# Moving casts to GpSimd and mirrors away from it in a fused attention and Fourier-mixing kernel

## The chip, the cores and the metric

The kernel runs on one core of one Trainium2 chip. The metric is the device time of one execution in microseconds (us). A core has five engines that run their own instruction streams in order: TensorE (PE: matmuls and transposes, its weight loads shown as PEld), VectorE (DVE), ScalarE (ACT), GpSimd (POOL) and SyncE (SP), which only issues transfers here. They wait for each other by semaphores. Transfers between the chip's memory (HBM) and the on-chip buffer (SBUF) run on 16 DMA engines, fed by queues: q1 holds what SyncE issues, q10 what ScalarE issues, q0 what GpSimd issues. Matmuls write to PSUM, a small accumulator memory that the kernel uses in banks.

## The reference

Inputs: q, k and v of 4 batches x 8 heads x 768 positions x 64, in float32, two weights (512x2048 and 2048x512), and two numbers, 8 global and 96 local positions.

```
scores = q @ k.T / sqrt(64)                     # per batch and head
keep   = (column < 8) or (0 <= row - column < 96)
scores = scores - slope[head] * distance        # then -1e9 where not keep
a      = softmax(scores)
x      = (a @ v), heads side by side            # 4 x 768 x 512
u      = x + real(fft(fft(x, axis=1), axis=2))
un     = (u - mean(u)) / sqrt(var(u) + 1e-6)    # over the last axis
out    = u + relu(un @ w_ch1) @ w_ch2
```

## The kernel before

**Two layers of work.** For each batch there is an attention part and a mixing part, and after them a large feed-forward part that fills TensorE. Heads are taken in pairs (hp 0 to 3); the number n = 4 * batch + hp names a pair through the whole kernel, so q4, k4 and v4 are batch 1's first loads and k7 its last k.

Attention, per pair: `load` reads q, k and v as float32 (L354 to L394). `cast_qk` (L400 to L421) casts q and k to float16, 128x768 each, with heads and positions put in another order. `trans` (L489) turns the cast tiles with 12 TensorE transposes ("pt") and copies them to SBUF as qkT (L505, L507). Two small GpSimd copies, kG (L512), take the global columns out of qkT. `score` (L519) has three units per pair ("sc"): four matmuls, an exponential on ScalarE (L566) into "er", a multiplication with a mask on VectorE (L581). `cast_v` (L465) casts v on GpSimd (L469). `v_global`, `glob` and `av` make the weighted sums ("pvg", "pgl", "pav"), which VectorE divides into x (L691, L692).

Mixing, per batch: `bounce` (L701) writes x to HBM (xd) and reads it back in another row order (xr). `fold_s` and `fold_d` (L723 to L856) fold x for the transform on VectorE. `y_unit` (L861) makes the transform along positions ("py"), copied out as zy (L896, L898). `mirror` (L911) makes copies with reversed columns of five parts of zy: r0 (three instructions, L916 to L918) and rn 0 to 3 (one each, L929 on ScalarE or L931 on GpSimd). `u_unit` (L952) makes the transform along features ("pu"), adds xr into u (L984), normalizes it (un, L1004 or L1006), squares it for the variance (L1013) and computes one over the deviation on GpSimd ("rstd", L1020 and L1021). `nt_unit` (L1025) transposes un ("ptu").

Feed-forward, per chunk c of 256 rows (three per batch): `ph_unit` (L1056) is the first product, 8 units of 8 matmuls, each copied out with the relu by ScalarE or VectorE (L1072, L1073); `pg_unit` (L1079) is the second, 16 matmuls of 512 columns per 128-row tile, closed by a VectorE step (L1100) that scales and adds u, and by the store (L1105).

**Buffers.** q and k of all pairs but batch 0's first three share three buffers (qs), v has two (vs), the cast tiles two (qk), xr and zy one each. A load waits until the cast has freed the buffer. Attention and mixing units share two PSUM banks ("xx"); the ph and pg units have two each.

**What sets the order.** The order is written by a planner in the kernel, `Plan` (L18 to L152), when the program is built. It keeps an expected time for each engine and each result. A piece of work for VectorE, ScalarE, GpSimd or SyncE is handed to `later` with its `ways`: the engines that may do it, each with an expected duration. `run` (L115) takes TensorE's units from four lists (mixing, attention, ph, pg), always the one that can start first, and places the other engines' work by the expected times. The hardware then executes every engine's list in that fixed order, whatever the real times are. `LAND` (L343) gives the planner the expected landing times of batch 1's and 2's loads. `fill` (L313) puts empty matmuls into early gaps.

**Queues around the change.** SyncE issues all loads of q, k and v, and from chunk 6 on the stores. Batch 1's loads wait until batch 0's xr has been issued; batch 2's wait for `hold` (L1188): a tiny transfer out of the second weight, which SyncE can issue only when that part of the weight (w2[1]) has landed. GpSimd issues the eight weight loads (`wload`, L1174), w1[0] to w1[3] and w2[0] to w2[3], between its casts and copies.

Of the kernel before, what the change touches and what calls it, by code (L numbers as in the profile page):

```python
# [14 lines left out]
P = 128  # L15
# [143 lines left out]
def act(n):  # L159
    return 0.19 + n / 1200.0  # L160
# [15 lines left out]
def kernel(  # L176
# [136 lines left out]
    def fill(until):  # L313
# [15 lines left out]
        for i in range(n):  # L329
# [10 lines left out]
    TT = {}  # L340


    LAND = {4: (43.5, 43.3, 47.3), 5: (51.6, 55.5, 54.0), 6: (57.4, 60.9, 59.2), 7: (65.9, 67.0, 64.9),  # L343
            8: (79.4, 81.6, 84.8), 9: (86.6, 91.0, 88.2), 10: (92.8, 96.3, 94.8), 11: (100.0, 102.5, 98.4)}

    def landed(n, w):
        def then(t):
# [5 lines left out]
    def load(b, hp, which):  # L353
        n = HP * b + hp  # L354
        h0 = 2 * hp
        vtag, vi = ("u", hp) if b == 0 else ("vs", n - HP)
        stage[("vs", n)] = (vtag, vi)
        gate = [("hold", b)] if b == 2 else [("xri", 0)] if b == 1 else []
        if which == "v" and b == 0:
            def run():  # L360
                t = buf(vtag, vi, [P, 2 * NS, Dh], FP32, 1)
                stage[("v", n)] = t
                qk_dma(t.rearrange("p (j t) d -> p j (t d)", t=2), v, b, h0)
            pl.later([("SP", 0.45, run)], free(vtag, vi), 0.0, [("ld", "v", n)], dma=1.34)
        elif which == "v":
            def run():
                t = buf(vtag, vi, [P, 2 * NS, Dh], FP32, 1)
                stage[("v", n)] = t
                src = v[b, h0:h0 + 2].rearrange("h s d -> (h s) d").rearrange("(n m t) d -> t m n d", m=64, t=2)
                for t2 in range(2):  # L370
                    nc.sync.dma_start(t[64 * t2:64 * t2 + 64], src[t2])
            pl.later([("SP", 0.9, run)], free(vtag, vi) + gate, 0.0, [("ld", "v", n)], lat=(0.0, 4.0, 6.0, 5.0)[b], dma=2.45, then=landed(n, 2))
        elif b == 0 and hp < 3:
            cell = {}

            def run(cell=cell):
                cell[0] = buf("hT", hp, [P, 2, NS, 2 * Dh], FP32, 2)
                for w, src in enumerate((q, k)):
                    qk_dma(cell[0][:, w], src, b, h0)
            pl.later([("SP", 0.9, run)], free("hT", hp), 0.0, [("ld", "qk", n, w) for w in range(2)], dma=2.68,  # L380
                     then=lambda t: pl.tok.__setitem__(("ld", "qk", n, 0), t - 1.34))
            for w in range(2):
                cast_qk(b, hp, w, lambda w=w, cell=cell: cell[0][:, w], ("hT", hp))
        else:
            for w, src in enumerate((q, k)):
                cell = {}
                i = 2 * (n - 3) + w

# [11 lines left out]
    def cast_qk(b, hp, w, src, freed):  # L400
        n = HP * b + hp

        def cast(on):
            if n not in qk16:
                qk16[n] = buf("qk", n, [P, 2, NS, 2, Dh], FP16, 1)
            d = qk16[n][:, w]
            s = src().rearrange("p (h i) (t d) -> p h (i t) d", h=2, t=2).rearrange("p h j d -> p j h d")
            if on == "ACT":
                A(d, s, AF.Copy)  # L409
            elif on == "DVE":  # L410
                V.tensor_copy(d, s)
            else:
                nc.gpsimd.tensor_copy(d, s)
        ways = [("ACT", act(768), lambda: cast("ACT")), ("DVE", dve2(768), lambda: cast("DVE"))]
        if b:
            ways = [("ACT", act(768), lambda: cast("ACT")), ("POOL", 1.6, lambda: cast("POOL"))]
        else:
            if hp:
                ways = ways[1:2] if w else [("POOL", 0.85, lambda: cast("POOL"))]
        pl.later(ways, [("ld", "qk", n, w)] + free("qk", n), 0.0, [("qk", n, w)], [("free",) + freed],  # L420
                 rank=1 if b else 0)  # L421
# [488 lines left out]

    def mirror(b):  # L911

        def r0():
            rev = buf("rev0", b, [P, 2, 2, P], FP16, 2)
            src = T[("y", b)][:, 4]
            nc.gpsimd.tensor_copy(rev[:, 0, :, 0:1], src[:, 0, :, 0:1])  # L916
            nc.gpsimd.tensor_copy(rev[:, 0, :, 1:P], src[:, 0, :, P - 1:0:-1])
            nc.gpsimd.tensor_copy(rev[:, 1], src[:, 1, :, ::-1])  # L918
            Y[(b, 0, 3, "r")], Y[(b, 3, 3, "r")] = rev[:, 0], rev[:, 1]
        pl.later([("POOL", 1.0, r0)], [("y", b, 0, 3), ("y", b, 3, 3)] + free("rev0", b), 0.0,  # L920
                 [("y", b, 0, 3, "r"), ("y", b, 3, 3, "r")], [("free", "zy", 2 * b + 1)])

        def rn(n, on):
            if n == 0:
                T[("rev", b)] = buf("ww", IW(b, NA(b) + 1), [P, 4, 2, 2, P], FP16, 1)
            rev = T[("rev", b)]
            d, y = rev[:, n], T[("y", b)][:, n, :, :, ::-1]
            if on == "ACT":
                A(d, y, AF.Copy)  # L929
            else:  # L930
                nc.gpsimd.tensor_copy(d, y)  # L931
            for a in range(2):
                Y[(b,) + YG[n // 2][2 * (n % 2) + a] + ("r",)] = rev[:, n, a]
        for n in range(4):
            ys = YG[n // 2][2 * (n % 2):2 * (n % 2) + 2]
            pl.later([("ACT", act(512), lambda n=n: rn(n, "ACT")), ("POOL", 1.0, lambda n=n: rn(n, "POOL"))],
                     [("y", b) + y for y in ys] + free("ww", IW(b, NA(b) + 1)) + [("rv", b, n - 1)][:n], 0.0,
                     [("y", b) + y + ("r",) for y in ys] + [("rv", b, n)],
                     [("free", "zy", 2 * b + 1)] if n == 3 else [])
# [139 lines left out]
    def pg_unit(c, t, part):  # L1079
# [26 lines left out]
            pl.later([("ACT" if c < 6 else "SP", 0.45, st)], [("ob", i)], 0.0, [], [("free", "ob", i)], lat=1.6, dma=0.7)  # L1106
        PG.append((needs, ("pg",) if part == 0 else None, run))


    def dma_const(dst, src, us, tok, needs=()):  # L1110
        pl.later([("SP", 0.45, lambda: nc.sync.dma_start(dst, src.ap()))], needs, 0.0, [tok], lat=0.2, dma=us)

    with tc.manual_schedule():
# [74 lines left out]
        def hold(n, src):  # L1188

            nc.sync.dma_start(dr.tile([1, 32], FP16, tag=f"hold{n}", name=f"hold{n}", bufs=1), src)  # L1190
        pl.later([("SP", 0.5, lambda: hold(2, w2[0:1, 4, 0:32]))], [("w2", 1)], 0.0, [("hold", 2)])
        for b in range(B):
            if b:
                for hp in range(HP):
# [96 lines left out]
```

## Time and profile before

| what | us |
|---|---|
| median of 7 runs (lowest to highest) | 280.87 (280.07 to 283.28) |
| the profiled execution, whole | 282.54 |
| its span, first to last instruction | 280.8 |
| PE busy, share of the span | 265.8, 95% |
| DVE busy | 178.9, 64% |
| ACT busy | 151.2, 54% |
| POOL busy | 61.3, 22% |
| q and k casts on ACT (L409), 20 times | 16.6 in all, 0.839 each |
| q and k casts on POOL (L413), 5 of qs | 5.3 in all, 1.057 each |
| v casts on POOL (L469), 12 times | 10.9 in all, 0.909 each |
| mirror copies rn on POOL (L931), 6 times | 4.0 in all, 0.668 each |
| last VectorE step of a tile (L1100) | 0.747 |
| last store, issue to landing | 2.1 |

How to read it: busy times overlap, and a share is an average over stages with different limits. The page has several views: busy times by engine; the span in 40 equal slices of 7.02 us, a digit for the busy tenths in each; the DMA queues; the chain of waits, followed back from the last instruction; the costliest groups of instructions. Further views of the same trace show instructions in order of time, busy time by stages, and what landed when. A row such as `L409 ACT ACTIVATE qk<-qs` names the source line, the engine, the operation and the tiles written and read. Line numbers are those of the kernel before.

### The profile page before, as it was taken

What the parts mean: (1) busy time and instruction counts of PE and PEld (TensorE: products, weight loads), DVE (VectorE), ACT (ScalarE), POOL (GpSimd) and SP (SyncE); (2) the same over time, 40 slices, a digit from 0 to 9 for tenths busy, and PEclk for the clock granted to TensorE, in tenths of its full rate; (3) what the DMA queues carried; (4) which work ended last, traced back from release to release, by engine and by line L of the source; (5) the groups of instructions that cost most, each with busy time, mean ns of one, the idle gap of its engine ahead of it and who ended that gap; (6) DMA issues with size and microseconds to landing.
All of it is one profiled execution on the core that took longest, in us unless ns stands there. A gap on an engine that the chain in (4) does not pass through costs nothing.

```text
span 280.8 us, 6109 instructions
## 1 busy us (share of the span) xinstructions
PE 265.8 (95%) x2505; PEld 179.6 (64%) x2505; DVE 178.9 (64%) x356; ACT 151.2 (54%) x245; POOL 61.3 (22%) x118
## 2 busy tenths in 40 slices
PE   8789998998699999999999999999999999999994
PEld 3445577886456556786885678666677577757441
DVE  4676937786357999976899565767895525111121
ACT  2878257892571368888547765684157346324000
POOL 1573535254112053262012102011002020000000
PEclk9999999999599999999999999999999999999999
DMA  7999799999989989982045110100540101010111
GB/s 220 291 284 288 170 266 204 210 212 216 235 154 193 307 242 245 239 175 74 1 121 163 75 40 0 41 0 4 153 146 37 41 37 40 0 75 20 57 75 75
DMA packets 63101, 38.10 MB, mean 136 GB/s; under 512 B 20450, under 2 KB 58594, under 8 KB 62946
## 3 DMA queue, kind: packets, MB, share of 16 engines
q1 hardware_dynamic: 51458, 25.66, 38.7%
q10 hardware_dynamic: 7392, 7.87, 9.2%
q0 software_dynamic: 4224, 4.19, 9.1%
q8 instruction: 19, 0.31, 0.5%
q14 instruction: 8, 0.07, 0.1%
HBM read 32.47 MB, written 9.44 MB: 149 GB/s over the span
## 4 chain that ended last, share of the span: by engine, by line
PE 72%; DMA 14%; DVE 5%; SPq 3%; issue 2%; ACT 2%; POOL 1%; ACTq 0%; POOLq 0%
PE pg L1089 29%; PE ph L1066 26%; DMA qs<-in_k_dram 7%; PE sc L543 3%; PE pav L672 3%; PE pt L498 3%; DMA vs<-in_v_dram 3%; SPq L398 2%; DMA qs<-in_q_dram 2%; PE pu L963 2%; DVE x L692 2%; PE py L879 2%; PE ptu L1035 1%; PE py L882 1%; DMA xd<-x 1%
## 5 line engine op out<-in xcount | busy, mean ns | idle before, releaser
L1066 PE MATMUL ph<-unT,w 128*128 128x256 f16 x768 | 95.5, 276 | 0.0
L1089 PE MATMUL pg<-w,hT 128*128 128x512 f16 x384 | 90.9, 379 | 0.0
L1066 PEld LDWEIGHTS <-w 128*128 128x128 f16 x768 | 72.9, 99 | 16.5 <-issue 4.4
L1072 ACT ACTIVATE hT<-ph 128x512 f16<-128x512 f32 x56 | 33.4, 597 | 47.9 <-PE ph L1066 47.6
L1089 PEld LDWEIGHTS <-hT 128*128 128x128 f16 x384 | 35.9, 98 | 35.7 <-issue 1.5
L1100 DVE SCALAR_TENSOR_TENSOR ob<-pg,sm,u 128x512 f32<-128x512 f32 x24 | 17.9, 747 | 41.6 <-PE pg L1089 41.3
L566 ACT ACTIVATE er<-sc 128x992 f16<-128x992 f32 (+2 forms) x42 | 38.1, 922 | 8.8 <-PE sc L543 6.6
L1073 DVE TENSOR_SCALAR hT<-ph 128x512 f16<-128x512 f32 x40 | 27.6, 690 | 18.9 <-PE ph L1066 18.6
L581 DVE TENSOR_TENSOR ex<-er,mk 128x992 f16<-128x992 f16 (+2 forms) x42 | 26.7, 647 | 4.4 <-ACT er L566 4.3
L984 DVE SCALAR_TENSOR_TENSOR u<-pu,xr 128x512 f32<-128x512 f32 x24 | 15.7, 686 | 8.6 <-PE pu L963 8.6
L409 ACT ACTIVATE qk<-qs 128x768 f16<-128x768 f32 x20 | 16.6, 839 | 7.7 <-DMA qs<-in_k_dram 6.3
L512 POOL COPY kG<-qkT 64x8 f16<-64x8 f16 x32 | 10.5, 327 | 41.9 <-DVE qkT L507 32.1
L498 PE MATMUL pt<-ident,qk 128*128 128x128 f16 x192 | 14.3, 227 | 5.1 <-ACT er L566 4.1
L692 DVE TENSOR_TENSOR x<-pav,rc 128x512 f16<-128x512 f32 (+1 forms) x27 | 17.1, 632 | 0.9
L543 PE MATMUL sc<-qkT 64*128 64x256 f16 (+1 forms) x192 | 16.6, 263 | 0.5 <-ACT v L460 0.4
L498 PEld LDWEIGHTS <-qk 128*128 128x128 f16 x192 | 12.4, 102 | 7.3 <-issue 5.1
L672 PEld LDWEIGHTS <-ex 128*128 128x128 f16 x352 | 15.0, 97 | 2.5 <-DVE rc L691 0.4
L672 PE MATMUL pav<-v,ex 128*128 128x65 f16 x352 | 16.1, 193 | 0.0
L896 ACT ACTIVATE zy<-py 128x512 f16<-128x512 f32 (+1 forms) x13 | 9.7, 759 | 11.8 <-DVE eA L829 5.2
L469 POOL CAST v<-vs 128x768 f16<-128x768 f32 x12 | 10.9, 909 | 22.9 <-DMA vs<-in_v_dram 22.8
L1013 ACT ACTIVATE un<-un 128x512 f16<-128x512 f16 x24 | 14.9, 622 | 1.7 <-PE ptu L1035 1.2
L507 DVE COPY qkT<-pt 128x1536 f16<-128x1536 f16 x14 | 13.4, 954 | 1.6 <-PE pt L498 1.4
(104 smaller groups left out, 290.6 us busy)
## 6 DMA issues: line engine op xcount, KB each, us to landing
qs<-in_q_dram SPq DMA_DIRECT2D x13, 384.0 KB, 7.1
qs<-in_k_dram SPq DMA_DIRECT2D x13, 384.0 KB, 6.4
vs<-in_v_dram SPq DMA_DIRECT2D x24, 192.0 KB, 7.5
w<-in_moe_w_ch_dram POOLq DMA_DIRECT2D x8, 512.0 KB, 10.4
out_dram<-ob ACTq DMA_DIRECT2D x12, 256.0 KB, 2.3
out_dram<-ob SPq DMA_DIRECT2D x12, 256.0 KB, 2.0
xd<-x ACTq DMA_DIRECT2D x12, 192.0 KB, 3.4
xr<-xd ACTq DMA_DIRECT2D x6, 384.0 KB, 3.8
```

What stands on the lines that cost most here:

```text
L409: A(d, s, AF.Copy)
L498: nc.tensor.transpose(o[:, j % 2], src[:, w, j].rearrange("p h d -> p (h d)"), idn)
L543: nc.tensor.matmul(pa[:, s, c0:c0 + cw], TT[n][lo:lo + 64, 1, i * P:(i + 1) * P], TT[n][lo:lo + 64, 0, i * P:i * P + cw], start=(not inps) ...
L566: A(mine(), cut(pa), AF.Exp, 0.0, 0.125)
L581: VT(o, mine(), m, op=ALU.mult)
L672: nc.tensor.matmul(po[:, jj, hh * 65:(hh + 1) * 65], lhsT, v16[b % 2][:, i, h, 0:65], start=(jp == 0 and a == 0), stop=(a == len(ops) - 1) ...
L692: VT(X[b][:, 2 * jp:2 * jp + 2, first * Dh:(first + nh) * Dh].rearrange("p j (h d) -> p j h d", d=Dh), pv[:, :, :, 0:Dh], rc.to_broadcast( ...
L1066: nc.tensor.matmul(ph[:, a * CH:(a + 1) * CH], w1[:, d, jb * P:(jb + 1) * P], UNT[c][:, d, :], start=(d == 0), stop=(d == ND - 1))
L1072: pl.later([("ACT", act(512), lambda: A(dst, ph, AF.Relu)), ("DVE", dve(512), lambda: V.tensor_scalar_max(dst, ph, 0.0))], [], e, [("h", c ...
L1073: ("DVE", dve(512), lambda: V.tensor_scalar_max(dst, ph, 0.0))],
L1089: nc.tensor.matmul(pg, HT[c][:, jb, t * P:(t + 1) * P], w2[:, jb, :], start=(jb == 0), stop=(jb == NJ - 1))
L1100: V.scalar_tensor_tensor(cell[0], pg, MV[c][:, t, 3:4], UT[c][:, t, :], op0=ALU.mult, op1=ALU.add)
```

## The change

Four edits, and new expected landing times for the planner.

1. The casts of q and k of batches 1 to 3 have GpSimd as their only way, with an expected 1.0 us. Before, ScalarE or GpSimd could be chosen.
2. The mirrors of batches 1 to 3 lose GpSimd as a way: r0 may go to ScalarE or VectorE, rn to ScalarE or VectorE. Batch 0 keeps what it had.
3. Batch 3's loads wait for a second `hold`, a tiny transfer out of batch 1's xr, queued on SyncE.
4. The last 128-row tile of the last chunk is done in two halves of 256 columns (`pg_last`): 16 matmuls, a VectorE step and a store each.

```diff
-    LAND = {4: (43.5, 43.3, 47.3), 5: (51.6, 55.5, 54.0), 6: (57.4, 60.9, 59.2), 7: (65.9, 67.0, 64.9),
-            8: (79.4, 81.6, 84.8), 9: (86.6, 91.0, 88.2), 10: (92.8, 96.3, 94.8), 11: (100.0, 102.5, 98.4)}
+    LAND = {4: (46.0, 46.0, 47.0), 5: (51.5, 55.5, 54.0), 6: (56.5, 60.0, 59.0), 7: (66.5, 68.0, 64.0),
+            8: (79.5, 81.0, 83.5), 9: (86.3, 89.5, 87.5), 10: (90.7, 95.7, 93.8), 11: (99.5, 101.5, 98.5)}
...
-        gate = [("hold", b)] if b == 2 else [("xri", 0)] if b == 1 else []
+        gate = [("hold", b)] if b > 1 else [("xri", 0)] if b == 1 else []
...
         if b:
-            ways = [("ACT", act(768), lambda: cast("ACT")), ("POOL", 1.6, lambda: cast("POOL"))]
+            ways = [("POOL", 1.0, lambda: cast("POOL"))]
...
-        def r0():
+        def r0(cp):
...
-            nc.gpsimd.tensor_copy(rev[:, 0, :, 0:1], src[:, 0, :, 0:1])
-            nc.gpsimd.tensor_copy(rev[:, 0, :, 1:P], src[:, 0, :, P - 1:0:-1])
-            nc.gpsimd.tensor_copy(rev[:, 1], src[:, 1, :, ::-1])
+            cp(rev[:, 0, :, 0:1], src[:, 0, :, 0:1])
+            cp(rev[:, 0, :, 1:P], src[:, 0, :, P - 1:0:-1])
+            cp(rev[:, 1], src[:, 1, :, ::-1])
...
-        pl.later([("POOL", 1.0, r0)], [("y", b, 0, 3), ("y", b, 3, 3)] + free("rev0", b), 0.0,
+        pl.later([("ACT", 1.0, lambda: r0(nc.scalar.copy)), ("DVE", 0.8, lambda: r0(V.tensor_copy))] if b else
+                 [("POOL", 1.0, lambda: r0(nc.gpsimd.tensor_copy))], [("y", b, 0, 3), ("y", b, 3, 3)] + free("rev0", b), 0.0,
...
-                nc.gpsimd.tensor_copy(d, y)
+                (V if on == "DVE" else nc.gpsimd).tensor_copy(d, y)
...
-            pl.later([("ACT", act(512), lambda n=n: rn(n, "ACT")), ("POOL", 1.0, lambda n=n: rn(n, "POOL"))],
+            pl.later([("ACT", act(512), lambda n=n: rn(n, "ACT")), ("DVE", 0.7, lambda n=n: rn(n, "DVE")) if b else ("POOL", 1.0, lambda n=n: rn(n, "POOL"))],
...
+    def pg_last(c, t, half):
...
+        cols = slice(half * 256, half * 256 + 256)
...
+            for jb in range(NJ):
+                nc.tensor.matmul(pg[:, 0:256], HT[c][:, jb, t * P:(t + 1) * P], w2[:, jb, cols],
+                                 start=(jb == 0), stop=(jb == NJ - 1))
...
+                V.scalar_tensor_tensor(cell[0], pg[:, 0:256], MV[c][:, t, 3:4], UT[c][:, t, cols],
+                                       op0=ALU.mult, op1=ALU.add)
...
+            pl.later([("SP", 0.45, lambda: nc.sync.dma_start(out[b].rearrange("(m r) d -> m r d", r=6)[:, rs, cols], cell[0]))],
+                     [("ob", i)], 0.0, [], [("free", "ob", i)], lat=1.6, dma=0.4)
...
         pl.later([("SP", 0.5, lambda: hold(2, w2[0:1, 4, 0:32]))], [("w2", 1)], 0.0, [("hold", 2)])
+        pl.later([("SP", 0.5, lambda: hold(3, XR[1][0:1, 5, 0:32]))], [("xr", 1)], 0.0, [("hold", 3)])
...
             for t in range(2):
+                if (c, t) == (NP * B - 1, 1):
+                    pg_last(c, t, 0)
+                    pg_last(c, t, 1)
+                    continue
```

Since the planner orders everything anew, the instruction lists of all engines differ from batch 1 on. The parts that the prediction uses: on GpSimd, between batch 0's rstd and batch 1's last kG, the list is now kG 4 (first half), cast q5, kG 4 (second), rstd 1, cast v5, cast k5, cast q6, cast v6, kG 5 (first), cast k6, kG 5 (second), w2[0], rstd 2, w2[1], cast v7, kG 6, w2[2], w2[3], cast q7, cast k7, kG 7. On SyncE, batch 1's loads come in the order q4, k4, v4, q5, v5, k5, q6, v6, k6, t1 (a table), v7, q7, k7, hold 2; before, q6 came ahead of k5. On TensorE the transposes of pair 4 stand after two ph units instead of before the first, and those of pair 7 have the third score unit of pair 6 and batch 1's global-value unit ahead of them instead of behind. The number of matmuls of each kind is the same, but for the last tile.

More of the change, by code (lines that the diff above doesn't have):

```diff
@@ L1107, in pg_unit, with run, add @@
         PG.append((needs, ("pg",) if part == 0 else None, run))
+    def pg_last(c, t, half):
+        b, pr = divmod(c, NP)
+        rs = PAIRS[pr][t]
+        cols = slice(half * 256, half * 256 + 256)
+        def run(start, ring):
+            pg = bank(ring, f"pg_{c}_{t}_{half}")
+            for jb in range(NJ):
+                nc.tensor.matmul(pg[:, 0:256], HT[c][:, jb, t * P:(t + 1) * P], w2[:, jb, cols],
+                                 start=(jb == 0), stop=(jb == NJ - 1))
+            e = pl.pe(mm_us(256, NJ), start)
+            i = HP + 2 * c + t + half
+            cell = {}
+            def add():
+                cell[0] = buf("ob", i, [P, 256], FP32, 1)
+                V.scalar_tensor_tensor(cell[0], pg[:, 0:256], MV[c][:, t, 3:4], UT[c][:, t, cols],
+                                       op0=ALU.mult, op1=ALU.add)
+            pl.later([("DVE", dve(256), add)], [("rstd", c)] + free("ob", i), e, [("ob", i)], ring=ring, rank=0)
+            pl.later([("SP", 0.45, lambda: nc.sync.dma_start(out[b].rearrange("(m r) d -> m r d", r=6)[:, rs, cols], cell[0]))],
+                     [("ob", i)], 0.0, [], [("free", "ob", i)], lat=1.6, dma=0.4)
+        PG.append(([("h", c, j) for j in range(NJ // 2)], ("pg", "ph"), run))
     def dma_const(dst, src, us, tok, needs=()):
```

## The prediction

> I call a load and its cast by pair of heads, counted through the batches (n = 4 x batch + pair): k7 is the k of the last pair of batch 1. w2[0] to w2[3] are the four loads of the second weight.
>
> **What bounds the kernel now.** First the page's slices of 7 us: TensorE is busy nearly throughout, with one hole and one stretch of low clock in the same place, slices 10 to 12.
>
> ```profile
> PE   8789998998699999999999999999999999999994
> ...
> PEclk9999999999599999999999999999999999999999
> DMA  7999799999989989982045110100540101010111
> ```
>
> After that place TensorE doesn't stop until the end, so time won or lost there arrives at the end one for one, unless another wait takes it back. Second, the table by stages (us; then busy us and instruction counts of PE, PEld, DVE, ACT, POOL; granted clock; DMA share; GB/s), cut at the hole:
>
> ```profile
> 64.00:69.17 5.17, 5.17 (x49) 3.49 (x47) 3.92 (x6) 2.03 (x3) 2.68 (x5) 1.00 1.20 217
> 69.17:72.93 3.76, 0.00 (x1) 0.00 (x1) 0.02 (x1) 1.78 (x3) 0.00 (x0) 0.78 1.23 203
> 72.93:78.28 5.35, 5.35 (x37) 3.48 (x38) 2.77 (x4) 2.10 (x3) 0.73 (x2) 0.52 1.10 241
> ```
>
> TensorE does nothing for 3.76 us and then works 5.35 us at 0.52 of its clock. Third, the chain of waits there (start, us, what):
>
> ```profile
> 58.18 12.95 DMA qs<-in_k_dram
> ...
> 71.26 0.64 issue
> 71.90 0.99 ACT er L566
> ...
> 72.93 1.44 PE pt L498 x12
> 74.37 1.71 PE ph L1066 x8
> 76.07 0.43 PE sc L543 x4
> 76.51 1.77 PE ph L1066 x8
> ```
>
> The load of k7 takes 12.95 us to land. ScalarE stands in front of its cast (71.15 to 71.99) and so does the exponential of the scores behind it in the same queue; TensorE's transposes of pair 7 wait for the cast and for the PSUM bank which that exponential frees. At full clock the same pieces take 0.67, 0.98, 0.32 and 0.98 in the chain of 80 to 96 us, so the low clock costs 0.77 + 0.73 + 0.11 + 0.79 = 2.40. Together 3.76 + 2.40 = 6.16 us.
>
> Why is k7 late? Fourth view, the DMA queues by windows (q1 is SyncE's, with q, k and v; q0 is GpSimd's, with the weights; packets, MB, share of the 16 engines). From 60 to 62 us:
>
> ```profile
> q1 hardware_dynamic: 886, 0.37, 119.0%
> ```
>
> and from 62 to 70 us:
>
> ```profile
> q0 software_dynamic: 1238, 1.24, 92.9%
> q1 hardware_dynamic: 964, 0.48, 27.3%
> ```
>
> q1 moves 0.185 MB/us alone, and 0.06 MB/us once q0 runs. GpSimd issues w2[0] at 58.64, and q0's bytes appear 3.3 us later; from then k7 crawls.
>
> **Part 1, the casts.** 24 casts of batches 1 to 3 now stand 20 on ScalarE (L409, 839 ns each) and 4 on GpSimd (L413, 1057 ns mean over five, 0.83 when alone). All go to GpSimd: ScalarE loses 20 x 0.84 = 16.8 us, GpSimd gains 16.6 to 21. Two things follow at the hole. (a) The exponential no longer stands behind k7's cast. (b) In the new program GpSimd's queue is: cast v6, half of pair 5's small copy (kG), cast k6, other half, w2[0], rstd 2, w2[1], cast v7, kG 6, w2[2], w2[3], cast q7, cast k7. So w2[0] can't go before k6 has landed and is cast. k6 is issued at 52.28 and takes 7.3: 59.58; cast 0.83, copy 0.2: w2[0] at 60.6, 2.0 us later than now; w2[1] after 0.8 + 0.9 (rstd) at 62.3, 2.1 later. The 2.0 us give q1 2.0 x 0.185 = 0.37 of the 0.48 MB that it now moves beside the weights; the other 0.11 at 0.06 MB/us take 1.8. k7 lands near 62 + 2.0 + 1.8 = 65.8 (issued as now), and its cast, behind w2[3]'s issue near 66, ends by 67 to 68. TensorE reaches the transposes of pair 7 at 69.17 plus what the new order puts ahead of them (scores 0.43 and a global-value unit 0.31) = 69.9. No wait: -3.76 and -2.40. From the other side: with k7 at 71.1 as now, the cast ends at 72.0 to 72.4.
>
> Does the rest of that queue keep pace? SyncE reuses three qs buffers, so each cast gates a load: q5's cast must end before k6's issue at 52.28. Ahead of it stand rstd 0 and the first kG 4, which needs the transposes of pair 4; these now stand after two ph units, and their copy ends near 50.4, so q5 is cast by 51.5: 0.8 us to spare. k7's buffer needs q6's cast: landed at 55.5, done by 56.4, against 58.18. First and smallest margin: 0.8; who waits if it goes: k6, v7, q7, k7, in SyncE's order.
>
> The Trainium skill, "GPSIMD Engine Reference" (Key points), says VectorE is about twice as fast at elementwise work. Here the row is a ScalarE row against a GpSimd row for the same 128x768 cast, 0.84 against 0.83 to 1.06, so by the row nothing is lost. By the page's factor a cast would be near 1.7, the four q and k casts ahead of w2[0] would be 3.4 late, 2.6 of it past the margin, and the sum at the end of this text would be near 277.9.
>
> **Part 2, the mirrors of batches 1 to 3.** Off GpSimd: 3 x (0.19 + 0.40 + 0.40) and 4 x 0.67 = 5.6 us. In the new order VectorE takes r0 of batches 1 and 2 and one rn of batch 1, ScalarE the rest, 3 rn more than now at 0.62 each and one r0. VectorE has no reversed copy in this trace: bounds 0.28 (plain 256-element f16 row) to 0.69 (512 from PSUM), I take GpSimd's own 0.40. ScalarE hides its part in the 16.8 us freed. VectorE's part lands where VectorE is fullest:
>
> ```profile
> 84.30:95.60 11.30, 11.30 (x130) 6.90 (x128) 9.75 (x23) 2.37 (x5) 2.05 (x2) 1.00 1.03 233
> 95.60:118.40 22.80, 22.42 (x198) 13.95 (x195) 21.94 (x49) 16.25 (x24) 7.85 (x15) 1.00 1.06 250
> ```
>
> 31.7 busy of 34.1: 2.4 us free. A GpSimd cast also slows VectorE:
>
> ```profile
> 88.38 0.56 DVE L739 TENSOR_TENSOR eA<-x 128x768 f16<-128x768 f16 x1
> ...
> 88.40 1.22 POOL L413 CAST qk<-qs 128x768 f16<-128x768 f32 x1 [1.91 <-DMA qs<-in_k_dram]
> ...
> 88.86 1.18 DVE L740 TENSOR_TENSOR eA<-x 128x768 f16<-128x768 f16 x1
> ```
>
> L740 undisturbed is 0.55 (at 96.12): +0.63; L812 +0.43 (1.39 against 0.96), L581 +0.40: mean 0.48. Eight more casts stand in this stretch (q8 to k11 and q12, one stands there now): 8 x 0.48 = 3.8. Mirrors 0.99 + 0.67 = 1.7; pair 8's copy of transposes comes back to VectorE, 0.95; two y and two unT copies go to ScalarE, -2 x 0.68 - 2 x 0.42 = -2.2. Sum +4.2 us. Cover: 2.4 us free, and the new order has 8 more pg matmuls (1.73) and a score unit (0.43) before batch 1's first ph unit: 4.6. It fits by 0.4; I take +0.5 (0 to 3.5).
>
> The Trainium skill, "SBUF — State Buffer" (SBUF: two separate sides), speaks against the change: GpSimd and VectorE share one port pair that is locked for a whole instruction, and the loser blocks entirely. The row shows 0.63 lost beside a 1.22 us cast. By the page a cast may cost VectorE its whole length; the sum would then be that of the second rival below, 282.9, and by the row it stays at 275.3.
>
> **Part 3, the hold of batch 3's loads.** One small DMA on SyncE that waits for batch 1's xr; behind it on SyncE stand batch 3's loads alone, and behind q12's and k12's casts on GpSimd small copies and rstd 3. xr is issued at 100.33 and lands 7.3 later, at 107.6; its user (L984 at 112.30) comes 4.7 later behind other VectorE work, so an earlier landing gains 0. Batch 3's loads begin at 100.3 now and its first transposes run at 143.7: some 30 us of cover; without it the price would be the wait for xr, up to 7.3. I take 0.
>
> **Part 4, the last tile in halves.** Matmuls: 32 x 0.109 against 16 x 0.216, +0.05. The last VectorE step falls from 0.75 by 0.27 (L692: 0.69 for 512, 0.42 for 256). The last store, 2.1 to landing, is half: gain 0 to 0.5, I take 0. Sum -0.2.
>
> **New order elsewhere.** Between 40 and 60 us TensorE now idles 20.00 - 18.61 = 1.39; I take +0.3 for the moved transposes (-1 to +1.5). LAND's new numbers only change the order already read.
>
> **Sum.** -6.16 - 0.2 + 0.5 + 0.3 = -5.6. The profiled execution took 282.54 with a span of 280.8; the median of the runs is 280.87, so I take the difference from the median: 275.3. Own range: with all low bounds 280.87 - 6.16 - 0.7 - 1 = 273.0, with all high ones 275.3 + 3.0 + 1.2 = 279.5; 273.8 to 278.5, as bounds seldom meet.
>
> **Rivals.** *k7 lands no earlier* (the delay of w2 is eaten by loads issued late, the 0.8 us margin). TensorE then waits from 69.9 to 72.2, 2.3 instead of 3.76, -1.5. With the clock loss kept: 280.87 - 1.5 - 0.2 + 0.8 = 280.0; without it 277.6. For: q1 was saturated before 62. Against: GpSimd's order forbids w2[0] before k6's cast. That a 2.3 us pause lowers the clock is shown by no row; "TensorE: Matmul & The Clock Gate" (What's actually happening) gives an idle window of about 3.4 us, which would make it the lower number.
> *GpSimd and VectorE hold each other* (slower). Place: 84 to 118. If each of the eight casts costs VectorE its full 1.24 (the longest in the trace), it is late by 9.9 + 0.4 - 4.6 = 5.7, TensorE runs out of pg units in front of batch 1's ph, and a pause over 3.76 halves the clock again: 275.3 - 0.5 + 5.7 + 2.4 = 282.9. It turns the result from about 1.0 us per cast. For: 19.11 of 20 us busy from 100 to 120. Against: rows of 0.40 to 0.63.
> *The wait moves to w2*: its loads are issued later and the first pg unit, at 82.89 now, would come 4 to 6 us earlier, at 77 to 79; q0's last bytes now fall between 75 and 77 us. A 3 us delay beyond that, with lost clock: 275.3 + 3 + 2.4 = 280.7, without it 278.3; 279.5.
>
> **Chances.** Forecast 0.54, k7 0.16 (0.03 of it no change), VectorE 0.21 (0.03 no change), w2 0.09 (a third each way). 0.5% is 1.4 us, about what can be told. Faster 0.54 + 0.13 + 0.03 = 0.70, same 0.09, slower 0.21. Range 273.8 to 282.0: below lies 0.03, above most of the VectorE rival, 0.16.
>
> **What would show it.** No hole and clock 1.00 from 64 to 80 us; w2[0] issued after 60; k7's time to landing under 10 us; TensorE busy to within 1 us from 84 to 118; the last VectorE step near 0.48. I am wrong if a pause of over 3 us stands anywhere after 60 us, above all before batch 1's ph units.

## The result, and the profile after

The changed kernel takes 277.68 us (median of 12 runs, 276.34 to 278.42) against 280.98 for the kernel before (31 runs, 278.7 to 285.02): ratio 0.9889, 95% interval 0.9868 to 0.9911, 3.3 us faster. 275.3 was forecast, a gain of 5.6; the range held the time. The profiled execution of the changed kernel took 278.41 (span 276.6), 0.7 above its median, while that of before stood 1.6 above its own. The ratios leave out executions more than 1.5% above the fastest of their kernel, so a ratio can look better than the median of all runs beside it.

The page's slices of 6.9 us, after: TensorE, its granted clock and the DMA engines. The hole of slices 10 to 12 is gone and the clock stays up; shallow new dips stand in slices 14 and 31, near 93 and 211 us.

```profile
PE   8689899999999899999999999999998999999995
...
PEclk9999999999999999999999999999999999999999
DMA  7999889999999989950163011002520101010112
```

The table by stages at the place of the old hole and over the two later stretches (us; then busy us and counts of PE, PEld, DVE, ACT, POOL; granted clock; DMA share; GB/s):

```profile
64.00:69.17 5.17, 5.17 (x58) 3.78 (x56) 3.22 (x6) 4.65 (x8) 4.75 (x8) 1.00 1.21 211
69.17:72.93 3.76, 3.76 (x51) 2.79 (x48) 2.76 (x5) 1.38 (x4) 0.46 (x3) 1.00 1.24 206
72.93:78.28 5.35, 5.35 (x75) 4.01 (x72) 3.94 (x8) 3.78 (x5) 0.00 (x0) 1.00 1.19 258
...
84.00:118.00 34.00, 31.75 (x286) 19.83 (x284) 32.76 (x65) 16.91 (x29) 17.90 (x23) 1.00 1.12 271
200.00:270.00 70.00, 68.93 (x502) 45.84 (x500) 25.47 (x49) 25.21 (x48) 2.65 (x6) 1.00 0.13 49
```

From 64 to 78.28 TensorE doesn't stop, at full clock. But it now idles 34.00 - 31.75 = 2.25 us between 84 and 118, and 1.07 between 200 and 270, where before it lost 0.38 and nothing. GpSimd's queue at the place of the old hole, after: w2[0] goes behind k6's cast, and k7's cast ends at 69.26.

```profile
59.71 0.82 POOL L413 CAST qk<-qs 128x768 f16<-128x768 f32 x1 [0.31 <-DMA qs<-in_k_dram]
...
60.73 0.82 POOL L1205 DMA_DIRECT2D w<-in_moe_w_ch_dram  x1
...
68.37 0.89 POOL L413 CAST qk<-qs 128x768 f16<-128x768 f32 x1 [0.32 <-DMA qs<-in_k_dram]
```

What TensorE waited for after 60 us (engine, line; what it waited for; us, times, longest), after:

```profile
PE pt L498 <- ACT er L566: 1.1, 1, 1.1
PE py L879 <- DVE zy L898: 0.9, 1, 0.9
PE pu L964 <- ACT zy L896: 0.6, 1, 0.6
PE pu L964 <- DVE zy L898: 0.5, 1, 0.5
PE ptu L1036 <- ACT unT L1046: 0.2, 1, 0.2
```

Three waits in front of batch 1's first ph unit (1.1, 0.9, 0.2) and two near 208 us (0.6, 0.5). The chain of waits through the first stretch, after (start, us, what):

```profile
82.33 8.07 DMA qs<-in_q_dram
...
90.48 0.35 ACTq L1106
...
90.93 1.01 ACT er L566
...
91.98 0.83 PE pt L498 x12
...
94.92 0.94 DVE qkT L507
...
97.80 1.50 DVE eA L829
...
102.01 1.66 DVE ex L581 x2
103.67 0.61 DVE zy L898
...
104.33 0.27 PE py L879
```

Read it from the top: a store on ScalarE's queue (L1106) is issued in the instant in which a load of q lands, though its data was ready at 88.54; the exponential behind it starts at 90.93, TensorE's transposes wait for the PSUM bank which that frees, and from 94.92 to 104.28 the chain runs through VectorE.

The account of the two profiled executions, idle time of TensorE by stretch and the rest:

| | before | after | difference | forecast |
|---|---|---|---|---|
| 0 to 40 us | 5.35 | 5.85 | +0.50 | |
| 40 to 60 | 1.39 | 0.66 | -0.73 | +0.3 |
| 60 to 80, idle | 3.76 | 0 | -3.76 | -3.76 |
| low clock behind it | 2.40 | 0 | -2.40 | -2.40 |
| 80 to 120 | 0.38 | 2.25 | +1.87 | +0.5 |
| 200 to 270 | 0 | 1.07 | +1.07 | 0 |
| more, smaller matmuls | | | +0.05 | +0.05 |
| last matmul's end to the span's end | 4.08 | 3.33 | -0.75 | -0.27 |
| sum | | | -4.15 | -5.6 |

The spans differ by 280.8 - 276.6 = 4.2. The medians differ by 3.3. The first row is the spread of executions and not the change: the second profiles below have 5.84 for the kernel before and 5.46 for the changed one.

### The profile page after: what moved, and what is told of

Read it like the earlier page. It is cut to its first block, busy times and chain, and to the rows that moved or that the text cites. A ratio compares the mean times of both kernels' runs of the same rounds, so it can differ in the third digit from the quotient of the medians.

```text
span 276.6 us, 6147 instructions
## 1 busy us (share of the span) xinstructions
PE 263.5 (95%) x2521; PEld 180.1 (65%) x2521; DVE 182.1 (66%) x359; ACT 139.8 (51%) x236; POOL 76.2 (28%) x125
## 4 chain that ended last, share of the span: by engine, by line
PE 63%; DMA 14%; DVE 11%; SPq 3%; POOL 3%; issue 2%; ACT 2%; ACTq 0%; POOLq 0%; DVEq 0%
PE ph L1067 23%; PE pg L1090 21%; DMA qs<-in_q_dram 5%; PE pu L964 3%; DMA vs<-in_v_dram 3%; DMA w<-in_moe_w_ch_dram 3%; DMA qs<-in_k_dram 3%; SPq L398 3%; PE sc L543 2%; PE py L875 2%; PE pav L672 2%; PE pt L498 2%; DVE u L985 2%; DVE x L692 2%; PE ptu L1036 1%
## 5 line engine op out<-in xcount | busy, mean ns | idle before, releaser
L1090 PE MATMUL pg<-w,hT 128*128 128x512 f16 x368 | 87.2, 379 | 0.0
L1067 PEld LDWEIGHTS <-w 128*128 128x128 f16 x768 | 71.8, 98 | 15.4 <-issue 4.2
L1090 PEld LDWEIGHTS <-hT 128*128 128x128 f16 x368 | 34.8, 98 | 34.1 <-issue 1.2
L413 POOL CAST qk<-qs 128x768 f16<-128x768 f32 x25 | 23.6, 951 | 31.1 <-PE pt L498 13.2
L1021 POOL TENSOR_SCALAR sm<-sm 128x2 f32<-128x2 f32 x12 | 3.1, 259 | 87.5 <-ACT un L1014 87.2
L896 ACT ACTIVATE zy<-py 128x512 f16<-128x512 f32 (+1 forms) x15 | 10.5, 706 | 18.8 <-PE py L882 5.5
L498 PE MATMUL pt<-ident,qk 128*128 128x128 f16 x192 | 13.5, 220 | 2.3 <-ACT er L566 1.4
L507 DVE COPY qkT<-pt 128x1536 f16<-128x1536 f16 x15 | 14.3, 951 | 1.5 <-PE pt L498 1.3
L498 PEld LDWEIGHTS <-qk 128*128 128x128 f16 x192 | 11.4, 98 | 4.2 <-issue 1.4
```

What stands on the lines that cost most here:

```text
L498: nc.tensor.transpose(o[:, j % 2], src[:, w, j].rearrange("p h d -> p (h d)"), idn)
L1067: nc.tensor.matmul(ph[:, a * CH:(a + 1) * CH], w1[:, d, jb * P:(jb + 1) * P], UNT[c][:, d, :], start=(d == 0), stop=(d == ND - 1))
L1090: nc.tensor.matmul(pg, HT[c][:, jb, t * P:(t + 1) * P], w2[:, jb, :], start=(jb == 0), stop=(jb == NJ - 1))
```

## The experiments

Five questions: is the hole in the profile of before that of every run; what makes k7 late; what do the other parts of the change do; where do the 1.87 and the 1.07 us come from; and can they be had back. All ratios are against the kernel before on the same chip.

### The two kernels once more

The kernel before, unchanged:

> The kernel before, unchanged, profiled a second time. Its profiled execution took 282.54 us, 1.6 us more than the median of its timed runs (280.98), and the forecast took the hole of that one execution (3.76 us of waiting, 2.40 us of low clock) as the hole of every run. Theory A, the hole varies: an execution near the median has a pause of 2 to 3.4 us before the transposes of pair 7, and less or no low clock behind it; the gain of the change in the median is then smaller than in the two profiled executions by the same 1 to 2 us. Theory B, the hole is the same each time: again a pause of 3.5 to 4.0 us, again a stretch of about 5 us at half clock, and what is missing from the forecast gain was given back elsewhere.

It took 278.57 us (span 276.8), one execution. Its table by stages at the hole:

```profile
64.00:69.12 5.12, 5.12 (x48) 3.44 (x47) 3.90 (x6) 2.03 (x3) 2.24 (x4) 1.00 1.17 206
69.12:71.31 2.19, 0.01 (x2) 0.00 (x1) 0.03 (x1) 1.78 (x3) 0.00 (x0) 1.00 1.15 174
71.31:76.66 5.35, 5.35 (x60) 3.63 (x60) 3.84 (x6) 3.99 (x8) 0.73 (x2) 1.00 1.15 242
```

A pause of 2.19 us in place of 3.76, and the clock stays at 1.00: the same order of the same instructions loses 2.2 us here and lost 6.2 in the other execution. Theory A holds. The mean granted clock is on record for 54 more runs of before: the 19 with a clock of 0.996 or more have a median of 279.76 us, the 35 with less 281.66. So the low clock comes in about two runs of three, and they are 1.9 us longer. Of the changed kernel's 23 runs 21 have a clock of 0.996 or more (median 277.77). Where neither has the low clock the change is thus worth 2.0 us; the rest of the 3.3 comes from the runs of before that have it.

The changed kernel, unchanged:

> The changed kernel once more, unchanged, as the measure for the other kernels run beside it and to see how its waits vary. The median was 277.68 us of twelve runs; 277.2 to 278.2 us expected. In the profile: no pause over 1.2 us after 60 us, TensorE's waits of about 1.1 us near 91 us and of about 1.1 us near 208 us again if they are part of the kernel's order, another size at 91 us if the landing of a load decides it.

277.96 us (11 runs), ratio 0.9894 (0.9865 to 0.9923). Its profile (span 276.9) shows that the change doesn't end the wait for k7 in every execution, it shortens it. What TensorE waited for after 60 us:

```profile
PE pt L498 <- POOL qk L413: 1.6, 1, 1.6
PE py L879 <- DVE zy L898: 0.9, 1, 0.9
PE pu L964 <- ACT zy L896: 0.6, 1, 0.6
PE pu L964 <- DVE zy L898: 0.5, 1, 0.5
PE py L879 <- DVE ww L839: 0.3, 1, 0.3
```

k7 landed at 69.98 here and TensorE paused 1.58 us for its cast (expected: none over 1.2). The two waits near 208 us are there again, to a tenth; they belong to the order. The wait of 1.1 near 91 us is not, and from 84 to 118 us TensorE idles 1.38 in place of 2.25. The second profiles of the two kernels (spans 276.8 and 276.9) stand level: this pair of executions shows none of the gain, which lies in the longer executions of before.

### Is it the weights' traffic? Two mirror images

The kernel before, with w2[0] held back and no cast moved; ScalarE's order is that of before:

```diff
-            needs = [("ld", "qk", 3, 1)] if i == 0 else [("v", 1, HP - 2)] if i == 4 else [("wl", 5), ("v", 1, HP - 1)] if i == 6 else [("wl", 2), ("y", 0, 0, 3, "r")] if i == 3 else [("wl", i - 1)]
+            needs = [("ld", "qk", 3, 1)] if i == 0 else [("v", 1, HP - 2), ("qk", 6, 1)] if i == 4 else [("wl", 5), ("v", 1, HP - 1)] if i == 6 else [("wl", 2), ("y", 0, 0, 3, "r")] if i == 3 else [("wl", i - 1)]
```

> The kernel before with one more condition: the first load of the second weight on GpSimd's queue waits for the cast of k6. All casts stay on ScalarE and GpSimd as before, ScalarE's order is the same. Theory A, the weights' traffic makes k7 late: w2[0] is issued near 61 us instead of 58.6, k7 lands at 66 to 68 instead of 71.1, the pause of 3.76 us before the transposes of pair 7 falls under 1.0 us and the clock stays at 1.00; the whole takes 275 to 277.5 us, as much gain as the whole change or more, with no cast moved to GpSimd. Theory B, ScalarE's order makes it (the exponential stands behind k7's cast, which is left so here): the pause stays above 2.5 us, and the time stays at 280 to 281.5 us.

279.46 us (12 runs, 277.09 to 282.45), ratio 0.995 (0.9912 to 0.9989). By the time it is neither theory; the stages tell why:

```profile
60.00:80.00 20.00, 20.00 (x217) 14.06 (x215) 15.93 (x28) 14.23 (x21) 6.64 (x13) 1.00 1.14 203
96.00:100.00 4.00, 2.33 (x19) 1.38 (x19) 3.93 (x7) 1.07 (x2) 1.85 (x3) 1.00 1.19 298
100.00:106.00 6.00, 6.00 (x36) 3.38 (x35) 3.55 (x8) 4.37 (x7) 0.48 (x3) 0.72 1.12 248
```

w2[0] went at 61.97 and the hole is gone, with every cast still on ScalarE. But the time won brings TensorE sooner to another wait, 1.67 us at 96 to 100, and 6 us at 0.72 of the clock behind it (6 x 0.28 = 1.7). The chain there:

```profile
91.56 6.41 DMA xd<-x
98.07 0.34 ACTq L719
...
98.93 1.00 ACT er L566
99.98 0.27 PE sc L543
```

The bounced x takes 6.41 us to be written; ScalarE's queue stands at its reading (L719), and the exponential behind it is late. Theory A holds for the hole; of what was won, the next wait took 3.4 us in this execution. So holding w2[0] back is enough to close the hole, but not for the whole gain: by the medians this one move is worth 1.6 us (281.07 for before on the same chip).

The mirror image, the changed kernel with w2[0] ahead of k6's cast and all casts on GpSimd:

```diff
-                     [("w1" if i < 4 else "w2", i % 4)], lat=0.5, dma=2.8, rank=1 if i < 4 else 2,
+                     [("w1" if i < 4 else "w2", i % 4)], lat=0.5, dma=2.8, rank=1 if i < 4 else 0 if i == 4 else 2,
```

> The changed kernel with w2[0] put ahead of k6's cast on GpSimd's queue; nothing else is moved on any engine but that cast and the small copy of pair 5 behind it. It is the mirror image of the kernel before with w2[0] held back. Theory A, the weights' traffic makes k7 late: w2[0] goes at 59.3 us (behind v6's cast, which ends at 59.28 now) instead of 60.73, k7 loses 1.4 us of the queue alone, 1.4 x (0.185 - 0.06) = 0.18 MB, which take 2.9 us at 0.06 MB/us: it lands near 71 instead of 68.3, and TensorE pauses 1.5 to 2.5 us before the transposes of pair 7; the whole takes 279 to 281 us. Theory B, the exponential freed from its place behind k7's cast made the gain: no pause over 1 us, 277.3 to 278.1 us.

280.7 us over its six executions. They fall in two groups: three of 277.34 to 279.63, which alone are in the ratio of 0.9888 (0.9837 to 0.994), and three of 281.77 to 283.51, each at a mean clock of 0.994; 2 of the changed kernel's 23 runs are that low. The profile is of the second group (281.77). GpSimd's queue:

```profile
58.97 0.82 POOL L1205 DMA_DIRECT2D w<-in_moe_w_ch_dram  x1
59.80 0.84 POOL L413 CAST qk<-qs 128x768 f16<-128x768 f32 x1
...
66.28 0.82 POOL L413 CAST qk<-qs 128x768 f16<-128x768 f32 x1
70.95 0.83 POOL L413 CAST qk<-qs 128x768 f16<-128x768 f32 x1 [3.85 <-DMA qs<-in_k_dram]
```

w2[0] goes 1.8 us earlier than in the changed kernel, and k7 lands at 70.9 (71 expected); TensorE pauses 2.02 us (1.5 to 2.5 expected). That is theory A, in this execution; the three short ones have no profile.

The changed kernel with the casts given back to ScalarE and all else kept:

```diff
-            ways = [("POOL", 1.0, lambda: cast("POOL"))]
+            ways = [("ACT", act(768), lambda: cast("ACT")), ("POOL", 1.6, lambda: cast("POOL"))]
```

> The changed kernel with the q and k casts free again to go to ScalarE or GpSimd in batches 1 to 3 (21 go to ScalarE); mirrors, third hold, halves of the last tile and the list of landing times stay changed. On GpSimd w2[0] then waits for the small copy of pair 5 and for nothing of k6. Theory A, the time of w2[0] decides: the copy ends near 60.5 us here too, so w2[0] goes at 60 to 61 us, the pause before the transposes of pair 7 is under 1.5 us, 277.5 to 279.5 us. Theory B, the casts themselves had to leave ScalarE: a pause over 2 us again, 280 to 281.5 us.

279.13 us (10 runs), ratio 0.9929 (0.9891 to 0.9968): some 1.2 slower than with the casts. My premise was off: pair 5's copy came sooner than in the changed kernel, w2[0] went at 59.14, and k7 landed at 71.29. TensorE paused 1.45 us there for k7's cast and 0.67 more for the exponential behind it. The time fits theory A (277.5 to 279.5), the two pauses together theory B: alone it proves nothing. The profiles together (us):

| kernel | w2[0] issued | k7 issued | k7 landed | TensorE's pause | clock behind it |
|---|---|---|---|---|---|
| before, again | 57.87 | 58.13 | 69.50 | 2.19 | 1.00 |
| before | 58.64 | 58.18 | 71.13 | 3.76 | 0.52 |
| changed, w2[0] ahead of k6's cast | 58.97 | 58.58 | 70.90 | 2.02 | 0.71 |
| changed, casts given back | 59.14 | 58.30 | 71.29 | 1.45 + 0.67 | 1.00 |
| changed, again | 60.59 | 58.76 | 69.98 | 1.58 | 1.00 |
| changed | 60.73 | 58.88 | 68.3 | 0 | 1.00 |
| before, w2[0] held back | 61.97 | 58.52 | 64.3 | 0 | 1.00 |

In the seven other profiles of this study w2[0] goes at 59.7 to 62.2, and TensorE doesn't pause there. So all four profiles with w2[0] before 59.2 have a pause, and one of the ten with w2[0] later. Within each group the landing does not follow w2[0]: six of the seven others have the changed kernel's order up to here and w2[0] at 59.74 to 60.38, and k7 lands at 64.8 to 66.3, against 68.3 and 69.98 in the changed kernel's own two. What makes this spread is open. By these rows the casts matter by where they put w2[0]; ScalarE's queue, reason (a) of the prediction, makes a pause longer (the exponential of before ran behind k7's cast) but doesn't cause it.

### The parts of the change

The casts alone, on the kernel before, with the changed list of landing times:

```diff
-            ways = [("ACT", act(768), lambda: cast("ACT")), ("POOL", 1.6, lambda: cast("POOL"))]
+            ways = [("POOL", 1.0, lambda: cast("POOL"))]
```

> The kernel before with the casts alone on GpSimd and with the changed kernel's list of landing times; the mirrors stay where they were, there is no third hold, the last tile is whole. The order on every engine is the changed kernel's up to batch 1's mirrors, near 100 us. Theory A, the casts' order carries the gain and the rest of the change is worth only the last tile's part: no pause from 64 to 80 us, and 277.9 to 278.6 us. Theory B, the mirrors had to leave GpSimd for it: behind the casts on GpSimd's queue they come late, batch 1's first ph unit starts after 115 us instead of 113.5 in the changed kernel, and the whole takes 279.3 to 281 us. Theory C, the mirrors on VectorE and ScalarE cost the changed kernel what it lost between 84 and 118 us (1.8 us) and near 208 us (1.4 us): 275.5 to 277 us.

277.85 us (6 runs), ratio 0.9891 (0.9842 to 0.994): the same as the whole change, with no pause from 64 to 80 us, nearest to theory A. Mirrors, hold and halves are together worth nothing that can be told.

The last tile whole:

```diff
-                if (c, t) == (NP * B - 1, 1):
+                if False:
```

> The changed kernel with its last tile in one piece again. The forecast gave the halves 0.2 us: 277.9 us then. The two profiles say 0.75 (from the last matmul's end to the end of the span 4.12 us before and 3.31 after, less 0.05 of more matmuls): 278.4 us, with a tail of about 4.1 us in the profile. If it is 277.5 to 277.8 the halves are worth nothing.

278.2 us (12 runs), ratio 0.9897 (0.9863 to 0.993): 0.2 to 0.5 above the changed kernel's two medians, too little to be told by the times. The profiles are sharper: from the last matmul's end to the end of the span it is 3.99 us here and 4.06 to 4.08 in the four other profiles with a whole last tile, and 3.32 to 3.40 in the nine with halves. 0.7 us, in every pair.

Without the third hold:

```diff
-        gate = [("hold", b)] if b > 1 else [("xri", 0)] if b == 1 else []
+        gate = [("hold", b)] if b == 2 else [("xri", 0)] if b == 1 else []
-        pl.later([("SP", 0.5, lambda: hold(3, XR[1][0:1, 5, 0:32]))], [("xr", 1)], 0.0, [("hold", 3)])
```

> The changed kernel without the third hold: batch 3's loads no longer wait for xr of batch 1. The forecast gave the hold 0 us. 277.4 to 278.0 us then, with the loads of q12 and k12 issued before xr has landed; if those loads held up the bounced x, xr lands later than in the changed kernel, batch 1's first ph unit starts after 114.5 us and the time is 278.5 us or more.

277.65 us (6 runs), ratio 0.9887 (0.9845 to 0.9929). q12 is issued at 97.47 instead of 100.26 and batch 1's first ph unit starts at 111.6, no later than in the changed kernel (113.4). The hold is worth nothing that six runs can tell.

### The 1.87 us in front of batch 1's ph units

VectorE and GpSimd do hold each other. The timeline of the changed kernel around 100 us (start, us, engine, line, operation, out and in, count):

```profile
99.32 0.80 DVE L837 TENSOR_TENSOR ww<-eA 128x256 f16<-128x256 f16 x1
...
100.24 0.28 DVE L839 TENSOR_TENSOR ww<-eA 128x256 f16<-128x256 f16 x1
100.30 0.91 POOL L413 CAST qk<-qs 128x768 f16<-128x768 f32 x1 [0.33 <-DMA qs<-in_q_dram]
100.44 0.91 DVE L840 TENSOR_TENSOR ww<-eA 128x256 f16<-128x256 f16 x1
```

L839 and L840 are the same operation; the one that starts behind a cast's start takes 0.63 more. Over 84 to 113.5 us VectorE's instructions are together 4.0 us longer than the shortest of the same line and shape in that execution, and 5.2 longer than the shortest in all fourteen profiles; in before 2.2 and 2.3. To give batch 2's casts back:

```diff
-            ways = [("POOL", 1.0, lambda: cast("POOL"))]
+            ways = [("POOL", 1.0, lambda: cast("POOL"))] if b != 2 else [("ACT", act(768), lambda: cast("ACT")), ("POOL", 1.6, lambda: cast("POOL"))]
```

> The changed kernel with the casts of batch 2 (q8 to k11) free again to go to ScalarE or GpSimd; those of batches 1 and 3 stay on GpSimd. Theory A, the 1.8 us lost between 84 and 118 us are VectorE's, held up by GpSimd's casts (0.63 us each time one runs beside a fast f16 operation, 3.9 us there in the changed kernel against 2.1 before): the lengthening falls to 2 to 2.5 us, TensorE's idle time from 84 to 118 under 0.6 us, and the whole takes 276.0 to 277.0 us. Theory B, the casts go back in front of exponentials on ScalarE's queue, and what VectorE wins is lost there: 277.4 to 278.5 us.

277.44 us (6 runs), ratio 0.9876 (0.9829 to 0.9923). The lengthening fell to 2.3 as theory A has it, but TensorE still idles 2.3 us from 84 to 118, now mostly behind ScalarE. This is theory B, an exchange. Nor do the two go together elsewhere: the kernel without the third hold has 4.7 us of lengthening by the second count, near the changed kernel's 5.2, and only 0.88 us of idle time from 84 to 118.

The wait of 1.1 us at 91, by moving the store that stood in front of the exponential:

```diff
-            pl.later([("ACT" if c < 6 else "SP", 0.45, st)], [("ob", i)], 0.0, [], [("free", "ob", i)], lat=1.6, dma=0.7)
+            pl.later([("ACT" if c < 6 else "SP", 0.45, st)], [("ob", i)], 90.0 if (c, t) == (0, 1) else 0.0, [], [("free", "ob", i)], lat=1.6, dma=0.7)
```

> The changed kernel with one instruction moved: the store of the second tile of batch 0 stands behind two exponentials of pair 8 on ScalarE's queue instead of ahead of them. In the changed kernel the store is issued at 90.48 us, when the load of q10 lands (issued 82.33, 8.07 to land), though its data was ready at 88.54, and the exponential behind it starts at 90.93 with its scores ready at 89.1; TensorE then waits 1.08 us. Theory A: the exponential starts near 89.2, the wait is gone, and the whole is 0.7 to 1.1 us less, 276.6 to 277.0 us. Theory B: VectorE is the bound from 90 to 112 us and takes the time back: within 0.3 us of 277.7.

277.76 us (6 runs), ratio 0.9852 (0.9814 to 0.9889). ScalarE's timeline shows the move working:

```profile
86.51 1.27 ACTq L711 DMA_DIRECT2D xd<-x  x2
88.53 1.86 ACT L566 ACTIVATE er<-sc 128x992 f16<-128x992 f32 x2 [6.35 <-PE sc L543]
91.19 0.35 ACTq L1106 DMA_DIRECT2D out_dram<-ob  x1
```

The exponential starts at 88.53 instead of 90.93, and the wait at 91 is gone from this profile (idle time from 84 to 118: 1.04). That alone shows little, as the second profile of the changed kernel has no such wait either, with the store where it was. The median didn't move: theory B by the times, though six runs from 276.08 to 278.39 don't exclude a few tenths.

### The 1.07 us near 208 us

The changed kernel there, all engines:

```profile
208.10 1.15 ACT L930 ACTIVATE ww<-zy 128x512 f16<-128x512 f16 x2 [2.47 <-PE py L879]
...
209.16 1.00 ACT L896 ACTIVATE zy<-py 128x1024 f16<-128x1024 f32 x1
...
209.33 0.27 PE L964 MATMUL pu<-t,zy 128*128 128x128 f16 x2 [0.45 <-DVE zy L898]
...
210.22 0.96 PE L964 MATMUL pu<-t,zy 128*128 128x128 f16 x14 [0.61 <-ACT zy L896]
```

Two mirrors (L930), needed by TensorE only at 211.87, stand on ScalarE in front of the copy (L896) that TensorE needs next. Batch 3's mirrors alone back on GpSimd:

```diff
-        pl.later([("ACT", 1.0, lambda: r0(nc.scalar.copy)), ("DVE", 0.8, lambda: r0(V.tensor_copy))] if b else
+        pl.later([("ACT", 1.0, lambda: r0(nc.scalar.copy)), ("DVE", 0.8, lambda: r0(V.tensor_copy))] if b in (1, 2) else
...
-            pl.later([("ACT", act(512), lambda n=n: rn(n, "ACT")), ("DVE", 0.7, lambda n=n: rn(n, "DVE")) if b else ("POOL", 1.0, lambda n=n: rn(n, "POOL"))],
+            pl.later([("POOL", 1.0, lambda n=n: rn(n, "POOL"))] if b == 3 else
+                     [("ACT", act(512), lambda n=n: rn(n, "ACT")), ("DVE", 0.7, lambda n=n: rn(n, "DVE")) if b else ("POOL", 1.0, lambda n=n: rn(n, "POOL"))],
```

> The changed kernel with the mirrors of batch 3 alone back on GpSimd. In the changed kernel two of them (L930, 1.15 us) stand on ScalarE ahead of the copy that TensorE waits for near 208 us, and 1.07 us are lost there. Theory A: without them the wait of 0.61 us for ScalarE's copy goes, 0.45 for VectorE's cast may stay; the whole is 0.6 to 1.1 us less than the changed kernel, 276.6 to 277.1 us. Theory B: the copy waits for TensorE's own products, and GpSimd's slower mirrors are waited for instead: 277.4 to 278.2 us.

276.24 us (6 runs), ratio 0.9821 (0.9781 to 0.9862). The same place in its timeline:

```profile
206.28 1.02 ACT L896 ACTIVATE zy<-py 128x1024 f16<-128x1024 f32 x1 [0.28 <-PE py L882]
...
207.03 1.72 POOL L932 COPY ww<-zy 128x512 f16<-128x512 f16 x3 [25.61 <-PE py L879]
207.60 1.06 PE L965 MATMUL pu<-t,zy 128*128 128x128 f16 x16
```

The copy goes first, GpSimd, idle for 25.61 us, takes the mirrors beside it, and TensorE doesn't idle at all from 200 to 270 us. This is theory A, and more than it forecast (276.6 to 277.1): 1.4 to 1.7 below the changed kernel's two medians, of which the idle time explains 1.07. Both moves together:

> The changed kernel with the mirrors of batch 3 on GpSimd and the store of the second tile behind the two exponentials: the two moves that were tried singly (276.24 and 277.76 us). If both waits (1.1 us near 91, 1.1 us near 208) were lost for good, the sum is 277.7 - 2.2 = 275.5 us; if VectorE takes the first back between 92 and 112 us, 276.0 to 276.7 us, no less than with the mirrors alone.

276.21 us (6 runs, 274.6 to 277.15), ratio 0.9828 (0.9786 to 0.9871), beside 277.96 for the changed kernel on the same chip: 1.75 less, and no better than the mirrors alone. From 84 to 118 us TensorE idles 1.54 us in its profile, 1.3 of them for VectorE. In the medians this version and the simpler one above are shorter than both kernels.

## Why the prediction was right, and where its sizes were wrong

- **The cause of the hole** was right in reason (b), w2[0] held behind k6's cast. It went at 60.73 (60.6 forecast), w2[1] at 63.30 (62.3), and both mirror images show it. Reason (a) wasn't needed to close the hole: with ScalarE's order of before it went too. What (a) adds to the gain was not separated: w2[0] held back alone won 1.6 us, the casts 3.2.
- **The size of the hole was one execution's.** -3.76 and -2.40 were read off the profile and subtracted from the median, as if every run had them. The second profile has 2.19 and no low clock; the low clock is absent in 19 of 54 runs. "I take the difference from the median" is the step that failed: the profiled run stood 1.6 us above the median because its hole was deep.
- **k7's landing** was forecast at 65.8, with 2 to 3 us to spare before TensorE needs it. It was 68.3, and 69.98 in the second profile, while in six other profiles with the same order it was 64.8 to 66.3, so the forecast met the usual case and missed the spread. At 68.3 the cast ended at 69.26 and TensorE reached k7's transposes at 69.57: 0.3 was spare. In that execution k7 was issued 0.7 later than I took (58.88), and q1's bytes from 62 to 70 us were no more than before (0.50 MB against 0.48), though w2 came 2.1 us later.
- **84 to 118 us**, +0.5 taken, was +1.87, and it too is one execution's: +1.0 in the second profile. GpSimd's casts do lengthen VectorE, by less than priced: +1.8 to +2.9 in place of 3.8, since only casts beside a fast f16 operation cost anything (0.50 to 0.63 each). That this lengthening makes TensorE's idle time is not shown. What I left out is that the cover isn't one sum: VectorE idles 1.24 us of the 34 while TensorE idles 2.25, because each waits for the other in turn and for ScalarE, whose queue stood behind a store. "It fits by 0.4" can't be said of sums over 34 us.
- **The mirrors on ScalarE**, "hides its part in the 16.8 us freed", was wrong at one place, and it cost the most that could be had back: enough free time on the engine, but two mirrors in front of the one copy that TensorE waited for. +1.07 where I took 0.
- **The last tile**: VectorE's step 0.48 as forecast; of the store's gain, 0 to 0.5, I took 0, and it was 0.47. Right size, wrong end.
- **The reorder in 40 to 60 us**, +0.3 taken, was -0.73; **the hold**, 0, was 0.
- **The rivals.** *k7 lands no earlier* came half true in some runs. *GpSimd and VectorE hold each other* has its mechanism, at 0.63 a time and not 1.24 for each cast. *The wait moves to w2* did not come; in the kernel with w2[0] held back the wait moved, but to the bounced x.

The Trainium skill, "GPSIMD Engine Reference" (Key points), has VectorE about twice as fast at elementwise work. Batch 0 has casts of the same shape on VectorE (L411): 0.56 us, against 0.83 on GpSimd alone (up to 1.55 beside VectorE), so the factor is 1.5 here. The prediction put the page's factor on ScalarE's 0.84, and the 1.7 that this gave did not show. "SBUF — State Buffer" (SBUF: two separate sides) has the port pair locked for an instruction. The rows agree: L840 ended at 101.35, so with its own 0.28 it would have begun at 101.07, and the cast that it met ended at 101.21. All ten VectorE instructions that were lengthened by over 0.1 us between 84 and 118 us in this execution ended alike, as if begun 0.13 to 0.15 before the end of a cast that was running when they came. So what is lost is the rest of the cast, and not each time a whole one.

## What to carry to other kernels

Profile the kernel twice before pricing a stall: a wait for a transfer is a spread, not a number, and the profiled run may be its worst. Where two queues share the DMA engines, the place of one load in another engine's queue can open or close a pause, here of 2 to 4 us; that one move is quickly tried, and the next wait may keep part of what it wins. And free time on an engine hides a moved instruction only if nothing that sets the end stands behind it in the queue.

## What the runs showed of the hardware

- The low clock doesn't follow from a pause's length alone. After pauses of 2.19 and 1.58 us the clock stayed at 1.00, after 1.59 (98.39 to 99.98, w2[0] held back) it was 0.72 over the next 6 us, after 2.02 it was 0.71 from 73 to 78 us, after 3.76 0.52. "TensorE: Matmul & The Clock Gate" (What's actually happening), cited in the prediction, gives an idle window of about 3.4 us; these rows show the loss below it.
- Those means come from pieces at 0.50, each 3.41 us long: from 100.76 with w2[0] held back, from 72.53 with w2[0] ahead of k6's cast, from 20.81 in the kernel with the casts alone, and one of 6.83 from 71.27 in the kernel before. A piece of 3.41 costs 1.7 us while TensorE is busy, and lowers the mean clock of a run to 0.994, which is the commonest value below 0.996 among the runs of before (14 of 35).
- A store on ScalarE's queue, its data ready at 88.54, was issued at 90.48, when a load of q issued by SyncE landed (90.41). The trace's semaphores tell why: the transfers of SyncE and ScalarE take turns on eight semaphores, and the store has that load's and waits for it. In ten of the fourteen profiles the second store is issued within 0.1 us after the landing of the transfer ahead of it on its semaphore; in the other four its data came later. So a transfer can wait for one of another queue with which it has nothing else in common.
